# A cross network of six layers on one core: bank-to-bank PSUM copies, a second Strassen level in two products, and one rank list for the order

## The chip, the cores and the metric

One Trainium2 chip; the program runs on one of its cores. The metric is the device time in microseconds (us), as the median of several executions. A single-core program has no second die to compare with, so a run is called slow only when it lies over 1.5% above the fastest of the same kernel. "PE" is TensorE's matmul row in the trace, "PEld" its weight loads, "DVE" VectorE, "ACT" ScalarE, "SP" the queue that issues most DMAs.

## The reference

```python
B, F, D, L = 16384, 100, 16, 6
Din = min(F * D, 1024)                   # 1024
# x0: [B, Din], ws: [L, Din, Din], bs: [L, Din], all bfloat16
def reference(x0, ws, bs):
    x = x0
    for l in range(L):
        proj = jnp.einsum('bd,de->be', x, ws[l]) + bs[l]
        x = x0 * proj + x
    return x
```

Six products of 16384 x 1024 by 1024 x 1024, each followed by an elementwise step. The work is cut into 16 "pairs" of 1024 rows; a layer of a pair is called a **unit** here, so there are 96 units.

## The kernel before

Each unit is one product of two 1024 x 1024 matrices, done by Strassen's scheme in Winograd's form: seven products of 512 x 512 x 512 instead of eight, on sums of quadrants. The products are numbered 1 to 7; T1 to T4 are the sums of the quadrants of x, made by DVE; the sums of weights (5, 6, 7, 3) are made once, in pair 0, and kept in DRAM. One product is four *groups* (m = 0..3) of four matmuls with 512 columns. Product 2 is cut once more by the same scheme, into seven *inner groups* of four matmuls with 256 columns ("2i" are its sums of weights, "ti" its sums of x). This inner level saves an eighth of the columns of that one product.

```python
def group(pid, dst, m, start):                      # 4 matmuls, 512 columns each
    wt, rhs = weight(pid), rhs_of[pid]
    for k in range(KH):
        nc.tensor.matmul(dst[m][:], lhsT=wt[:, k, m * P:(m + 1) * P], rhs=rhs[:, k, :],
                         start=(start and k == 0), stop=(k == KH - 1), skip_group_check=True)
# ... one unit, in program order (cut) ...
for m in range(KH):                                  # product 1, bank pA[m]
    group(1, pA, m, True)
    evb(P1s[:, m, :], pA[m][:], 0, m)                # ACT: evict with bias
for m in range(KH):                                  # product 5, bank pX[m]
    group(5, pX, m, True)
    ev(P5s[:, m, :], pX[m][:])                       # ACT: evict
for m in range(KH):                                  # product 3 on top of product 5
    group(3, pX, m, False)
    evb(S53[:, m, :], pX[m][:], 0, m)
inner(1, 0, True); ev(i15[:, 0, :], pX[0][:])        # product 2, second level
inner(5, 1, True); ev(i15[:, 1, :], pX[1][:])
for m in (0, 1):
    group(6, pA, m, False)                           # product 6 on top of product 1
    ev(U2s[:, m, :], pA[m][:])
# ... inner 2, 6, 3, 7, 4 between the rest of products 6 and 7, 
#     each inner sum evicted by ACT and added by DVE ...
final(Q2[:], 0, 0)                                   # DVE: times x0, plus x
# ... product 7, product 4, their evictions, and the other three quadrants' finals ...
ti_next = emit_t(blk(xst, 1, 0))                     # DVE: inner sums for the next unit
emit_T(xst, Tn, (2, 3, 4))
```

PSUM has eight banks: `pA[0..3]` and `pX[0..3]`. Weights come through a ring of 14 tiles of 512 KB, eight loads per unit.

Of the kernel before, what the change touches and what calls it, by code (L numbers as in the profile page):

```python
# [1 line left out]

# [10 lines left out]
IDENT = mybir.ActivationFunctionType.Identity  # L13


@with_exitstack
def kernel(
# [18 lines left out]
    JB = PR // P  # L36

    KQ, HQ, NQ = KH // 2, H // 2, NB // 2

    const = ctx.enter_context(tc.tile_pool(name="const", bufs=1))  # L40
    dram = ctx.enter_context(tc.tile_pool(name="dram", bufs=1, space=bass.MemoryType.DRAM))
    x0t_pool = ctx.enter_context(tc.tile_pool(name="x0t", bufs=2))
    xst_pool = ctx.enter_context(tc.tile_pool(name="xst", bufs=2))
    t_pool = ctx.enter_context(tc.tile_pool(name="tp", bufs=1))
    ti_pool = ctx.enter_context(tc.tile_pool(name="tip", bufs=2))
    evi_pool = ctx.enter_context(tc.tile_pool(name="evi", bufs=1))
    ev_pool = ctx.enter_context(tc.tile_pool(name="evp", bufs=8))
    wring = ctx.enter_context(tc.tile_pool(name="wring", bufs=14))
    psum = ctx.enter_context(tc.tile_pool(name="ps", bufs=1, space=bass.MemoryType.PSUM))
    stage_ctx = ExitStack()  # L50
    w12_pool = stage_ctx.enter_context(tc.tile_pool(name="w12", bufs=2))
    xo_ctx = ExitStack()
    xo_pool = None

    Lc = dram.tile([L, 5, P, KH * H], BF16, name="Lc")
    CIDX = {5: 0, 6: 1, 7: 2, 3: 3, "2i": 4}
    pA = [psum.tile([P, NB], FP32, name=f"pA{i}") for i in range(KH)]
    pX = [psum.tile([P, NB], FP32, name=f"pX{i}") for i in range(KH)]

    def w_src(l, pid):  # L60
        wl = ws[l]
        if pid == 1:
            return wl[0:H, 0:H].rearrange("(k p) e -> p k e", p=P)
        if pid == 2:
            return wl[H:D, 0:H].rearrange("(k p) e -> p k e", p=P)
        if pid == 4:
            return wl[H:D, H:D].rearrange("(k p) e -> p k e", p=P)
        return Lc[l, CIDX[pid]].rearrange("p (k e) -> p k e", k=KH)

    ORDER = [1, 5, 3, 2, "2i", 6, 7, 4]  # L70
    all_keys = [(pr, l, pid) for pr in range(NPAIR) for l in range(L) for pid in ORDER]
    key_pos = {k_: i for i, k_ in enumerate(all_keys)}
    is_dma = lambda k_: not (k_[0] == 0 and k_[2] in CIDX)
    PREF = 11
    wtiles = {}
    state = {"next": 0}

    def prefetch_upto(n):
        while state["next"] < min(n, len(all_keys)):
            k_ = all_keys[state["next"]]  # L80
            if is_dma(k_) and k_ not in wtiles:
                wt = wring.tile([P, KH, H], BF16, name="wp")
                state["last_dma"] = nc.sync.dma_start(wt[:], w_src(k_[1], k_[2]))
                wtiles[k_] = wt
            state["next"] += 1
# [4 lines left out]
    def tt(out, in0, in1, op):  # L90
        nc.vector.tensor_tensor(out=out, in0=in0, in1=in1, op=op)  # L91

    def emit_T(xsrc, Ts, do):
        B11, B12, B21, B22 = blk(xsrc, 0, 0), blk(xsrc, 0, 1), blk(xsrc, 1, 0), blk(xsrc, 1, 1)
        for i in do:
            t_ = t_pool.tile([P, KH, NB], BF16, name=f"T{i}")
            Ts[i] = t_[:]
            if i == 1:
                tt(Ts[1], B12, B11, SUB)
            elif i == 2:  # L100
                tt(Ts[2], B22, Ts[1], SUB)
            elif i == 3:
                tt(Ts[3], B22, B12, SUB)
            else:
                tt(Ts[4], B21, Ts[2], SUB)

    def inner_w(t):
        v = t[:].rearrange("p q (k e) -> p q k e", k=KQ)
        return {5: v[:, 0], 6: v[:, 1], 3: v[:, 2], 7: v[:, 3]}

    def emit_t(B):
        q = lambda dh, n: B[:, dh * KQ:(dh + 1) * KQ, n * NQ:(n + 1) * NQ]
        t_ = ti_pool.tile([P, 4, KQ, NQ], BF16, name="ti")
        t1, t3, t2, t4 = (t_[:, i] for i in range(4))
        tt(t1, q(0, 1), q(0, 0), SUB)
        tt(t2, q(1, 1), t1, SUB)
        tt(t3, q(1, 1), q(0, 1), SUB)
        tt(t4, q(1, 0), t2, SUB)
        return {1: q(0, 0), 2: q(1, 0), 3: q(1, 1), 4: t4, 5: t1, 6: t2, 7: t3}

    combo_st = {}
    pending_saves = []

    def flush_saves():
        for (l_, pid_, t_) in pending_saves:
            si = nc.sync.dma_start(Lc[l_, CIDX[pid_]].rearrange("p (k e) -> p k e", k=KH), t_[:])
            if state.get("last_dma") is not None:
                tc.add_manual_dep(si.ins, state["last_dma"].ins.name,
                                  mybir.DependencyInfo(mybir.DependencyClass.NoSync, mybir.DependencyReason.DATA),
                                  reason="combo save behind the urgent weight loads")  # L130
        pending_saves.clear()

    def load_w12(l):
        st = combo_st.setdefault(l, {})
        if "w12" not in st:
            st["w12"] = w12_pool.tile([P, KH, H], BF16, name="w12")
            state["last_dma"] = nc.sync.dma_start(st["w12"][:], ws[l][0:H, H:D].rearrange("(k p) e -> p k e", p=P))
        return st["w12"]

    def emit_combo(l, pid):  # L140
        prefetch_upto(key_pos[(0, l, 4)] + 1)
        W11, W21, W22 = wtiles[(0, l, 1)], wtiles[(0, l, 2)], wtiles[(0, l, 4)]
        w12 = load_w12(l)
        t_ = wring.tile([P, KH, H], BF16, name="wp")
        if pid == 5:
            tt(t_[:], w12[:], W22[:], ADD)
        elif pid == 6:
            tt(t_[:], wtiles[(0, l, 5)][:], W11[:], SUB)
        elif pid == 3:
            tt(t_[:], W21[:], wtiles[(0, l, 6)][:], SUB)  # L150
        elif pid == 7:
            tt(t_[:], W11[:], w12[:], SUB)
        else:
            a11, a12 = W21[:, 0:KQ, 0:HQ], W21[:, KQ:KH, 0:HQ]
            a21, a22 = W21[:, 0:KQ, HQ:H], W21[:, KQ:KH, HQ:H]
            s = inner_w(t_)
            tt(s[5], a21, a22, ADD)
            tt(s[6], s[5], a11, SUB)
            tt(s[3], a12, s[6], SUB)
            tt(s[7], a11, a21, SUB)  # L160
        wtiles[(0, l, pid)] = t_
        pending_saves.append((l, pid, t_))

    wt0 = wring.tile([P, KH, H], BF16, name="wp")
    nc.sync.dma_start(wt0[:], w_src(0, 1))
    wtiles[(0, 0, 1)] = wt0
    load_w12(0)
    wt4 = wring.tile([P, KH, H], BF16, name="wp")
    nc.sync.dma_start(wt4[:], w_src(0, 4))
    wtiles[(0, 0, 4)] = wt4  # L170
    x0T_next = x0t_pool.tile([P, 2, KD, NB], BF16, name="x0T")
    for n in range(2):
        nc.sync.dma_start_transpose(out=x0T_next[:, n], in_=x0[n * NB:(n + 1) * NB, :])
    LK = L * KD
    b_bf = const.tile([P, LK], BF16, name="b_bf")
    nc.sync.dma_start_transpose(out=b_bf[:], in_=bs.rearrange("l (m p) -> (l m) p", p=P))
    b_all = const.tile([P, LK], FP32, name="b_all")
    prefetch_upto(8)
    nc.gpsimd.tensor_copy(b_all[:], b_bf[:])

    order_ctx = ctx.enter_context(tc.manual_schedule(engines={nc.tensor.engine, nc.scalar.engine, nc.vector.engine}))
    Tn = {}
    emit_combo(0, 5)
    emit_T(x0T_next, Tn, (1,))
    emit_combo(0, 6)
    emit_combo(0, 3)
    emit_combo(0, "2i")
    ti_next = emit_t(blk(x0T_next, 1, 0))
    emit_T(x0T_next, Tn, (2, 3))
    emit_combo(0, 7)  # L190
    emit_T(x0T_next, Tn, (4,))
    prefetch_upto(PREF)
    flush_saves()

    for pr in range(NPAIR):
        x0T = x0T_next
        xst = xst_pool.tile([P, 2, KD, NB], BF16, name="xst")
        last_pair = pr == NPAIR - 1
        xo_last = {"t": None, "regions": [], "xfin": None}

        def out_region(eh, n):
            if xo_last["t"] is None:
                xo_last["t"] = xo_pool.tile([P, 2, 2, KH, KH, P], BF16, name="xoS")
            ti = nc.sync.dma_start_transpose(out=xo_last["t"][:, eh, n].rearrange("p j k r -> p (j k) r"),
                                             in_=xo_last["xfin"][:, eh, n].rearrange("r j k p -> r (j k p)"))
            xo_last["regions"].append((eh, n))
            xo_last["tins"] = xo_last.get("tins", []) + [ti]

        for l in range(L):
            xsrc = x0T if l == 0 else xst  # L210
            Ts, ti = Tn, ti_next
            Tn = {}
            rhs_of = {1: blk(xsrc, 0, 0), 3: blk(xsrc, 1, 1), 4: Ts[4], 5: Ts[1], 6: Ts[2], 7: Ts[3]}
            bias_col = lambda eh, m: b_all[:, l * KD + eh * KH + m: l * KD + eh * KH + m + 1]
            last_layer = l + 1 == L
            combos_next = pr == 0 and not last_layer
            if combos_next:
                prefetch_upto(key_pos[(0, l + 1, 4)] + 1)
                load_w12(l + 1)
# [189 lines left out]
```

## Time and profile before

| kernel | median | runs |
|---|---|---|
| before | 2344.3 us | 2342.57 to 2345.61 (3 runs) |

The page's first part is the busy time of each engine, its share of the span, and the number of instructions.

```profile
span 2342.7 us, 31963 instructions
## 1 busy us (share of the span) xinstructions
PE 2277.5 (97%) x11668; PEld 1164.1 (50%) x11904; DVE 2003.2 (86%) x2160; ACT 1818.9 (78%) x2977; POOL 1.1 (0%) x5
```

The windows view, for the steady stretch: columns are the stretch, its length, then busy us and number of instructions for each engine, the granted clock, the share of the DMA engines' time, and GB/s.

```profile
200.00:2260.00 2060.00, 2048.66 (x10525) 1048.89 (x10736) 1775.60 (x1906) 1640.35 (x2685) 0.00 (x0) 1.00 0.75 222
```

PE is busy 99.4% of that stretch. The Trainium skill, "Trainium Kernel Development and Optimization", section "Performance Expectations", calls matmul busy time a bad metric for how close a kernel is to the roofline, because matmuls are pipelined. So I read starts instead. The timeline of before; each row is a start, a length, and merged like instructions:

```profile
1019.32 1.03 PE L233 MATMUL pX_92<-T_8766,wp 128*128 128x512 bf16 x4
1020.18 1.03 PE L233 MATMUL pX_93<-T_8766,wp 128*128 128x512 bf16 x4
...
1043.09 1.03 PE L233 MATMUL pX_92<-T_8891,wp 128*128 128x512 bf16 x4
```

Two groups of 512 columns start 0.86 us apart, although each row is 1.03 us long: the end of a matmul overlaps the next one. The same group of the next unit starts 23.77 us later. Groups cost 0.864 us and inner groups 0.437 us, from start to start, so 24 groups and 7 inner groups are 23.79 us: PE has no gap at all in a steady unit.

What isn't steady is the start. The waits of pair 0, from the timeline of PE (the bracket is the idle time before the row and what ended it):

```profile
11.80 1.86 PE L233 MATMUL pA_88<-x0T,wp 128*128 128x512 bf16 x4 [11.80 <-DMA x0T<-in_x_dram]
...
49.19 1.87 PE L233 MATMUL pA_88<-xst,wp 128*128 128x512 bf16 x4 [11.28 <-DVE xst L91]
```

Four more such waits, 0.95 to 3.6 us each, open the other layers of pair 0.

### The profile page before, as it was taken

Reading aid. Unit: us, or ns where it says so; the run is one execution under the profiler, and the core shown is the slowest. Engines: PE = TensorE matmul, PEld = TensorE weight load, DVE = VectorE, ACT = ScalarE, POOL = GpSimd, SP = SyncE. Lnnn points to the kernel's source line nnn. Section 1 sums busy time; section 2 is a strip of 40 time slices with the busy share of each in tenths; the row PEclk is TensorE's granted clock in tenths of the full one; section 3 lists DMA queues with packets and bytes.
Section 4 is the critical chain, followed back from the end, with each engine's and each line's share of the span. In section 5 each row is a group of like instructions: output and inputs, shape, how many; then the busy total and the mean of one; then the engine's idle time right before and its main releaser. Section 6 shows DMA issues by size and latency. Waiting matters only on the chain.

```text
span 2342.7 us, 31963 instructions
## 1 busy us (share of the span) xinstructions
PE 2277.5 (97%) x11668; PEld 1164.1 (50%) x11904; DVE 2003.2 (86%) x2160; ACT 1818.9 (78%) x2977; POOL 1.1 (0%) x5
## 2 busy tenths in 40 slices
PE   6989999999999999999999999999999999999996
PEld 2445555555454555555555545454555555554543
DVE  5998888888889788888888888888898888988886
ACT  4767777878787787778787878778777777787775
POOL 0000000000000000000000000000000000000000
PEclk8999999999999999999999999999999999999998
DMA  7659669595785958759586695967859578595853
GB/s 242 198 198 239 229 193 267 182 257 198 206 256 185 274 187 213 252 178 284 174 222 240 189 276 171 254 206 207 253 189 271 193 204 257 175 284 178 234 191 81
DMA packets 613837, 508.60 MB, mean 217 GB/s; under 512 B 399664, under 2 KB 552240, under 8 KB 613680
## 3 DMA queue, kind: packets, MB, share of 16 engines
q1 hardware_dynamic: 613680, 506.53, 72.5%
q8 instruction: 95, 1.56, 0.3%
q14 instruction: 62, 0.51, 0.1%
HBM read 390.07 MB, written 49.28 MB: 188 GB/s over the span
## 4 chain that ended last, share of the span: by engine, by line
PE 87%; DVE 10%; issue 1%; ACT 1%; SPq 1%; DMA 0%; DVEq 0%
PE pA_91 L233 13%; PE pA_88 L233 13%; PE pA_89 L233 13%; PE pA_90 L233 12%; PE pX_92 L245 7%; PE pX_94 L233 6%; PE pX_93 L233 6%; PE pX_95 L233 6%; PE pX_92 L233 6%; DVE ev L91 4%; PE pX_93 L245 3%; DVE xst L91 2%; PE pX_94 L245 2%; DVE wp L91 1%; DVE ti L91 1%
## 5 line engine op out<-in xcount | busy, mean ns | idle before, releaser
L233 PEld LDWEIGHTS <-wp 128*128 128x128 bf16 x9216 | 901.4, 98 | 1026.5 <-issue 55.1
L91 DVE TENSOR_TENSOR ev<-ev,x0T 128x2048 bf16<-128x2048 bf16 x384 | 469.8, 1223 | 9.9
L91 DVE TENSOR_TENSOR xst<-ev,xst 128x2048 bf16<-128x2048 bf16 x320 | 384.9, 1224 | 21.7 <-DVE ev L91 0.5
L91 DVE TENSOR_TENSOR ev<-ev 128x2048 bf16<-128x2048 bf16 x288 | 352.2, 1223 | 38.0 <-ACT ev L249 25.7
L245 PEld LDWEIGHTS <-wp 128*128 128x128 bf16 x2688 | 262.7, 98 | 133.2
L252 ACT ACTIVATE ev<-pA_88,b_all 128x512 bf16<-128x512 f32 x288 | 198.4, 689 | 69.9 <-PE pA_88 L233 65.7
L252 ACT ACTIVATE ev<-pA_90,b_all 128x512 bf16<-128x512 f32 x288 | 198.1, 688 | 34.9 <-PE pA_90 L233 33.4
L252 ACT ACTIVATE ev<-pA_91,b_all 128x512 bf16<-128x512 f32 x288 | 197.9, 687 | 34.0 <-PE pA_91 L233 34.0
L252 ACT ACTIVATE ev<-pA_89,b_all 128x512 bf16<-128x512 f32 x288 | 198.3, 689 | 25.6 <-PE pA_89 L233 1.8
L245 PE MATMUL pX_92<-ti,wp 128*128 128x256 bf16 x1152 | 172.8, 273 | 1.1
L249 ACT CAST ev<-pX_92 128x512 bf16<-128x512 f32 x192 | 112.3, 585 | 28.8 <-PE pX_92 L233 16.7
L233 PE MATMUL pA_88<-xst,wp 128*128 128x512 bf16 x320 | 83.0, 382 | 22.4 <-DVE xst L91 22.4
L252 ACT ACTIVATE ev<-pX_92,b_all 128x512 bf16<-128x512 f32 x96 | 66.0, 687 | 26.6 <-PE pX_92 L233 24.3
L233 PE MATMUL pA_89<-xst,wp 128*128 128x512 bf16 x314 | 83.2, 385 | 0.3
L233 PE MATMUL pA_91<-xst,wp 128*128 128x512 bf16 x315 | 82.3, 381 | 0.6
L233 PE MATMUL pX_94<-xst,wp 128*128 128x512 bf16 x320 | 82.1, 379 | 0.3
L233 PE MATMUL pA_90<-xst,wp 128*128 128x512 bf16 x306 | 81.7, 385 | 0.4
L233 PE MATMUL pX_93<-xst,wp 128*128 128x512 bf16 x308 | 80.5, 379 | 0.7
L233 PE MATMUL pX_95<-xst,wp 128*128 128x512 bf16 x308 | 80.5, 379 | 0.3
L233 PE MATMUL pX_92<-xst,wp 128*128 128x512 bf16 x306 | 80.3, 379 | 0.4
L252 ACT ACTIVATE ev<-pX_93,b_all 128x512 bf16<-128x512 f32 x96 | 66.0, 687 | 16.9 <-PE pX_93 L233 15.7
L252 ACT ACTIVATE ev<-pX_94,b_all 128x512 bf16<-128x512 f32 x96 | 66.0, 687 | 16.9 <-PE pX_94 L233 16.9
(2831 smaller groups left out, 3586.4 us busy)
## 6 DMA issues: line engine op xcount, KB each, us to landing
wp<-Lc SPq DMA_DIRECT2D x450, 512.0 KB, 4.3
wp<-in_ws_dram SPq DMA_DIRECT2D x288, 512.0 KB, 4.9
out_dram<-x0T SPq DMA_DIRECT2D x30, 1024.0 KB, 10.2
Lc<-wp SPq DMA_DIRECT2D x30, 512.0 KB, 6.3
out_dram<-xoS SPq DMA_DIRECT2D x4, 512.0 KB, 4.7
w_98<-in_ws_dram SPq DMA_DIRECT2D x1, 512.0 KB, 5.0
x0T<-in_x_dram SPq DMA_TRANSPOSE x32, 7.3
w_151<-in_ws_dram SPq DMA_DIRECT2D x1, 512.0 KB, 5.4
```

The source lines that it names most:

```text
L91: nc.vector.tensor_tensor(out=out, in0=in0, in1=in1, op=op)
L233: nc.tensor.matmul(dst[m][:], lhsT=wt[:, k, m * P:(m + 1) * P], rhs=rhs[:, k, :], start=(start and k == 0), stop=(k == KH - 1), skip_group ...
L245: nc.tensor.matmul(dst[:, m * NQ:(m + 1) * NQ], lhsT=wv[:, k, m * P:(m + 1) * P], rhs=ti[i][:, k, :], start=(start and m == 0 and k == 0), ...
L249: nc.scalar.copy(out=dst, in_=src)
L252: nc.scalar.activation(out=dst, in_=src, func=IDENT, bias=bias_col(eh, m), scale=1.0)
```

## The change

The intent has three parts.

1. **A second Strassen level inside two products, 5 and 2**, instead of in 2 alone. A steady unit then has 20 groups and 14 inner groups: 23.39 us of PE instead of 23.79. Pair 0 and the last unit drop the second level and have 28 groups, 24.18 us.
2. **Bank-to-bank copies.** A sum that two results share is copied by ACT from one PSUM bank to another (`F`, `f1`, `f2`), and PE goes on accumulating in both, so that DVE need not add the two.
3. **One rank list.** Every operation of PE, ACT and DVE has a rank, roughly its wanted start time in the unit; all operations are put out in order of rank as soon as what they depend on has been put out. Each engine works strictly in that order.

The diff, cut to its core (`...` marks cuts; the old unit's body is removed whole):

```diff
+R2 = ranks("""                      # two-level units; "name@rank"
+P1.0@0 5p1@.9 5p5@1.3 P1.1@1.7 P1.2@2.6 5p2@3.5 5p6@3.9 2p1@4.3 2p5@4.8 P1.3@5.2 5p3@6.1 5p7@6.5 2p2@7 2p6@7.4
+5p4@8 P6.1@8.5 2p7@9.4 P6.0@9.8 P3.1@10.7 2p3@11.5 2p4@12 P3.0@12.4 P6.3@13.3 P6.2@14.1 P3.3@15 P3.2@15.9
+P7.3@16.7 P7.0@17.6 P7.2@18.4 P7.1@19.3 P4.3@20.2 P4.0@21 P4.2@21.9 P4.1@22.8
+5e_p5@2 5f1@2.6 E1.1@3.1 E1.2@3.7 5e_c11@4.2 E1.0@4.7 5f2@5.3 2e_p5@5.7 2f1@6.4 5e_c12@6.8 5e_u3@7.3 2e_c11@7.8
+2f2@8.4 E1.3@8.9 F.1@9.6 5e_c21@10 2e_u3@10.5 F.0@11 2e_c12@12.2 E3.1@12.7 2e_c21@13.2 E3.0@13.7 F.3@14.3
+F.2@15.2 E3.3@16.1 E3.2@16.9 E7.3@17.8 E7.2@19.5 E7.0@20.1 E7.1@20.7 E4.0@22.1 E4.3@22.7 E4.2@23.2 E4.1@23.8
+T1@-1.1 5t13@.2 5t2@2.1 2t13@3.7 5t4@5.4 2t2@6.9 T2@7.2 T4@8.5 T3@9.6 2t4@10.8 5cc@11.1 2cc@12.8 Q1@13.9 Qm@15.1
+Qa@16.4 Ua@17.6 Um@18.9 Ux@20.2 Va@21.4 Wm@24.6 Wx@26 Vm@27.9 Vx@29.4
+""")
...
+SPAN2, SPAN0 = 23.4, 24.2           # length of a unit in ranks
...
-    wring = ctx.enter_context(tc.tile_pool(name="wring", bufs=14))
+    wring = ctx.enter_context(tc.tile_pool(name="wring", bufs=RING))      # 16
...
+    level1 = lambda u: units[u][0] == 0 or u == NU - 1
...
+                inner(5, b, True)                                # products 5 and 2, second level
+                copy(X + "e_p5", ip5[X][:], v3(b), [Xn[b]], [X + "ps"])
+                inner(1, a, True)
+                copy(X + "f1", pX[b][:], pX[a][:], [Xn[a]], [Xn[b]])   # bank to bank
+                inner(2, b, False)
+                copy(X + "e_c11", c(0, 0), v3(b), [Xn[b]], cn(0, 0))
+                inner(6, a, False)
+                copy(X + "f2", pX[b][:], pX[a][:], [Xn[a]], [Xn[b]])   # bank to bank
+                inner(3, b, False)
+                copy(X + "e_c12", iu[X][:, 0], v3(b), [Xn[b]], [X + "u0"])
+                inner(7, a, False)
+                copy(X + "e_u3", iu[X][:, 1], v3(a), [Xn[a]], [X + "u1"])
+                inner(4, a, False)
...
+        for m in range(KH):
+            xb = m if one else m % 2
+            group(f"P6.{m}", "6", pA[m], A[m], T[2], ["T2", A[m]], m, False)
+            copy(f"F.{m}", pX[xb][:], pA[m][:], [A[m]], [Xn[xb]])      # bank to bank
+            group(f"P3.{m}", "3", pX[xb], Xn[xb], B22, [XI[1, 1], Xn[xb]], m, False)
...
+    heap = [(ops[i][0], i) for i in range(len(ops)) if need[i] == 0]
+    heapq.heapify(heap)
+    while heap:
+        _, i = heapq.heappop(heap)
+        ops[i][1]()
...
```

Names: `P6.1` is group m = 1 of product 6, `E3.1` and `E7.1` are evictions, `F.1` a copy from bank to bank, `5p4` is the fourth inner product of product 5, `T2` a sum of quadrants, `5t4` an inner sum. `Q, U, V, W` are the four quadrants of the result; the suffixes are DVE steps: `a` or `1` adds, `m` multiplies by x0, `x` adds x (`Qa` is Q's last). Small parts of the change: x0 is loaded in four quarters at the start, 24 matmuls of zeros warm PE up (in the changed kernel's trace the first matmuls start 0.427 us apart, those from about 5.4 us on 0.216), the sums of weights are saved by the GpSimd queue.

The zeros do something else, too. The Trainium skill, "PSUM — Partial Sum Buffer", section "The four PSUM rules", says that writes of ScalarE neither set nor clear the bits which decide whether a matmul accumulates, that a matmul adds to what ScalarE wrote where an earlier matmul has left the bit set, and that zero is the only such start value that is safe either way. Accumulating on a copied bank relies on the bit being set.

## The prediction

> **What bounds it now.** The tensor engine's stream of columns. In the page's engine totals PE is busy 97% (DVE 86%, ACT 78%); by windows, 99.4% from 300 us to 2300 us. In the timeline a 4-matmul group of 512 columns starts every 0.864 us and an inner group of four 256-column matmuls every 0.437 us. One layer of one pair ("unit", 96 of them) is 24 and 7 of these: 23.79 us; the timeline shows 23.77 between like groups. 96 units are 2283 us. The other 60 us are: 11.8 us before the first matmul, 4 us of slow first groups, 22 us of PE waits on DVE at the starts of pair 0's layers (11.3, 0.95, 3.3, 3.3, 3.6), and 18 us after the last matmul. Steady units have none.
>
> **What changes.** 89 units get a second inner product in place of P5: 20 groups and 14 inner groups, 23.39 us (-0.40). Seven units (pair 0 and the last) go to one level: 28 groups, 24.18 us (+0.40). Net PE: -32 us (1.4%), all of it on the critical path, if PE stays the limit. Reordering should recover pair-0 waits.
>
> **What it adds per steady unit.** DVE: 15 adds of 2048 (1.14 us start to start, 1.26 where dependent), four of 1024 (estimated 0.60), four of 512 (0.34): about 22.1 us, 94% of 23.4. ACT: 16 biased evictions (0.58 to 0.69) and 18 copies (0.47 to 0.58): 18 to 21 us. Ten copies go from bank to bank; the Trainium skill, "ScalarE: Activation LUTs", in "Step-by-step: what each stage is for" says PSUM is the quicker destination; no trace here shows it yet. Weight loads: 9 of 512 KB instead of 8, 202 GB/s instead of 176; DMA busy rises from 72% to about 80%, with peaks at pair boundaries.
>
> **Why I don't grant the whole gain.** In rank order there is a loop across units: P6.1 waits for T2 of this unit; P6.1 to the start of P4.1 is 15 groups and 3 inner groups, 14.27 us; start of P4.1 to its eviction's end and Wm 1.81 us (1.07 + 0.69 + 0.05); then DVE, in order, Wm, 5t2, Wx, 2t13, Vm, 5t4, Vx, 2t2 before T2, 6.3 us; T2 to PE 1.37 us (1.23 + 0.14, as at the layer starts of pair 0). Sum 23.76 us, an estimate. So PE should wait 0.2 to 0.4 us before P6.1 in every unit; P6.3 -> copy -> P3.3 is also tight, within 0.1 us. I expect 23.5 to 23.8 us per unit, middle 23.68: nearly all of the PE saving turns into a wait.
>
> **Sum.** First matmul of data at 7 to 8 us; pair 0, near-balanced between PE and DVE (24.2 to 24.8 us a unit, plus about 8 us of startup waits), ends at about 163 us (182 before); 89 x 23.68 = 2107; last unit 24.5; tail 18.5. Total 2313 us, -1.3%; range 2288 to 2338. Chances: faster by over 2% 0.24, within 2% 0.74, slower by over 2% 0.02.
>
> **What would show it.** Steady period by the timeline; in the waits, PE pA <- DVE T2 of 0.2 to 0.4 us some 89 times; first-slice and pair-0 windows about 19 us shorter; the 1024-wide broadcast add near 0.69 us long; bank-to-bank copies at or below 0.585 us; no PE wait on DMA.
>
> **What would make it wrong.** Period 23.4 (loop hidden): 2289. The broadcast add losing its fast rate (1.2 us): DVE becomes the limit, 2330 or more. Weight loads late at pair boundaries: +1 us per pair. GpSimd saves slowing DVE in pair 0.

## The result, and the profile after

| kernel | median | runs | ratio to before, fast runs | 95% |
|---|---|---|---|---|
| before | 2344.31 us | 2342.57 to 2345.61 (4) | 1 | |
| changed | 2319.18 us | 2318.4 to 2320.84 (4) | 0.9894 | 0.988 to 0.9908 |

Ratios here and below are the mean time of one kernel's fast runs over that of the kernel before's in the same rounds, so not quite the ratio of the medians. The change wins 1.1%, clear of noise.

The same two views of the changed kernel:

```profile
span 2316.6 us, 34627 instructions
## 1 busy us (share of the span) xinstructions
PE 2272.3 (98%) x12674; PEld 1261.3 (54%) x12912; DVE 2102.9 (91%) x2218; ACT 1837.5 (79%) x3223; POOL 20.4 (1%) x41
```

```profile
200.00:2260.00 2060.00, 2048.18 (x11630) 1156.40 (x11846) 1901.77 (x2004) 1683.99 (x2962) 0.00 (x0) 1.00 0.80 243
```

PE's busy share of the steady stretch is 99.4% again, before and after, and after it hides a quarter of a microsecond of waiting in every unit. This fits the skill's warning: the row of a group here is longer (1.03 or 0.60 us) than its 0.864 or 0.437 us share of the stream, so a short wait falls inside the row and the profile doesn't count it. Only starts show it. The timeline of the changed kernel, one unit (its P1.0 starts at 1017.97):

```profile
1024.04 0.60 PE L287 MATMUL pX<-T,wp 128*128 128x256 bf16 x4
1024.48 0.60 PE L287 MATMUL pX<-ti,wp 128*128 128x256 bf16 x4
1025.04 0.60 PE L287 MATMUL pX<-x0T,wp 128*128 128x256 bf16 x4
1025.47 1.16 PE L287 MATMUL pX<-ti,wp 128*128 128x256 bf16 x8
1026.47 1.03 PE L189 MATMUL pA<-T,wp 128*128 128x512 bf16 x3
...
1041.60 1.03 PE L189 MATMUL pA<-xst,wp 128*128 128x512 bf16 x4
```

The rows are 5p3, 5p7, 2p2, then 2p6 and 5p4 together, P6.1, and P1.0 of the next unit, 23.63 us after this one's. 2p2 starts 0.56 us after 5p7 where 0.44 is its due; P6.1 starts 1.00 us after 2p6 where two inner groups take 0.87. I matched the single matmul records to the program's order through the weight loads (whose records are complete) and averaged over 70 steady units: the period is 23.655 us; **0.123 us is lost before 2p2, 0.120 us before 5p4, 0.012 us before P6.1**, 0.013 and 0.007 us before P3.3 and P3.2, nothing elsewhere. The rest, 23.38 us, is PE's own stream (23.39 by the sum above).

What 2p2 and 5p4 wait for is on ACT. Its timeline in the same unit:

```profile
1019.91 0.58 ACT L194 CAST ip<-pX 128x512 bf16<-128x512 f32 x1 [1.04 <-PE pX L287]
1020.52 0.57 ACT L194 COPY pX<-pX 128x512 f32<-128x512 f32 x1
1021.00 1.32 ACT L198 ACTIVATE ev<-pA,b_all 128x512 bf16<-128x512 f32 x2
1022.22 0.58 ACT L194 CAST ev<-pX 128x512 bf16<-128x512 f32 x1
1022.68 0.70 ACT L198 ACTIVATE ev<-pA,b_all 128x512 bf16<-128x512 f32 x1
1023.26 0.61 ACT L194 COPY pX<-pX 128x512 f32<-128x512 f32 x1
1023.78 0.61 ACT L194 CAST ip<-pX 128x512 bf16<-128x512 f32 x1
1024.42 0.57 ACT L194 COPY pX<-pX 128x512 f32<-128x512 f32 x1
1024.90 1.08 ACT L194 CAST iu<-pX 128x512 bf16<-128x512 f32 x2
```

These are 5e_p5, 5f1, E1.1 and E1.2, 5e_c11, **E1.0 at 1022.68**, 5f2, 2e_p5, 2f1, then 5e_c12 and 5e_u3. The bank copy 2f1 ends at 1024.99, and 2p2, which accumulates on that copy, starts at 1025.04. The eviction 5e_u3 ends at 1025.98; by the matched records 5p4, which goes on in the bank that it reads, starts on average 8.06 us into the unit, here 1026.03. ACT waits 1.04 us for PE before 5e_p5; from there to the end of this list it is never idle for more than about 0.03 us. This is no chance of one unit: over 80 steady units 2p2 starts 0.052 us after the end of 2f1, and 5p4 0.052 us after the end of 5e_u3, each within 0.001.

The other candidate is on DVE, which the prediction had named: T2, for which P6.1 waits. The timeline of DVE:

```profile
1018.89 1.23 DVE L103 TENSOR_TENSOR ev<-ev,x0T 128x2048 bf16<-128x2048 bf16 x1
...
1024.72 0.42 DVE L103 TENSOR_TENSOR ti<-x0T,ti 128x512 bf16<-128x512 bf16 x1
1025.05 2.55 DVE L103 TENSOR_TENSOR T<-x0T,T 128x2048 bf16<-128x2048 bf16 x2
```

Wm starts at 1018.89, 0.03 us after the eviction of P4.1 (a group of the unit before) has ended, as it does in nearly every steady unit. T2 (the first of the two merged) starts at 1025.05 and ends at 1026.27, and P6.1 starts at 1026.47. Where PE is seen to wait for T2, as in experiments 1 and 4, P6.1 starts 0.053 us after its end; here it is 0.089 us on average, so T2 comes some 0.04 us before it is needed. Two chains, then, end within some hundredths of a microsecond of each other.

Where the time came from, by the starts of unit 0, of unit 6 (pair 1) and of the last unit in both timelines:

| stretch | before | changed | difference |
|---|---|---|---|
| up to the first matmul of data | 11.8 | 8.4 | -3.4 |
| pair 0 (6 units) | 171.9 | 155.9 | -16.0 |
| 89 steady units | 2116.6 (23.78 each) | 2107.2 (23.68) | -9.4 |
| last unit | 23.8 | 24.3 | +0.6 |
| after the last matmul | 18.6 | 20.7 | +2.1 |
| span | 2342.7 | 2316.6 | -26.1 |

Three quarters of the gain is in the first 164 us. Of the 35 us that the second level saves on PE in the steady units (89 x 0.40), 9.4 us arrive.

### The profile page after: what moved, and what is told of

It reads as the page before. It is cut to its first block, busy times and chain, and to the rows that moved or that the text cites. A ratio compares the mean times of both kernels' runs of the same rounds, so it can differ in the third digit from the quotient of the medians.

```text
span 2316.6 us, 34627 instructions
## 1 busy us (share of the span) xinstructions
PE 2272.3 (98%) x12674; PEld 1261.3 (54%) x12912; DVE 2102.9 (91%) x2218; ACT 1837.5 (79%) x3223; POOL 20.4 (1%) x41
## 4 chain that ended last, share of the span: by engine, by line
PE 95%; DVE 2%; issue 1%; DMA 1%; SPq 0%; ACT 0%; DVEq 0%; ACTq 0%
PE pA L189 55%; PE pX L287 24%; PE pX L189 16%; DVE ev L103 1%; DVE xst L103 1%; SPq L384 0%; DVE T L103 0%; DMA Lc<-isum 0%; DMA x0T<-in_x_dram 0%; DVE wp L103 0%; ACT ev L198 0%; DVE ti L103 0%; SPq L391 0%; DVE isum L103 0%; ACT pX L194 0%
## 5 line engine op out<-in xcount | busy, mean ns | idle before, releaser
L189 PE MATMUL pA<-T,wp 128*128 128x512 bf16 x4512 | 1051.8, 379 | 5.5 <-DVE T L103 0.4
L198 ACT ACTIVATE ev<-pA,b_all 128x512 bf16<-128x512 f32 x1124 | 720.0, 688 | 187.9 <-PE pA L189 187.9
L103 DVE TENSOR_TENSOR ev<-ev,x0T 128x2048 bf16<-128x2048 bf16 x384 | 469.7, 1223 | 9.9 <-ACT ev L198 2.3
L287 PE MATMUL pX<-ti,wp 128*128 128x256 bf16 x2848 | 423.1, 272 | 1.6 <-DVE ti L103 1.6
L103 DVE TENSOR_TENSOR ev<-ev,ev 128x2048 bf16<-128x2048 bf16 x281 | 344.2, 1225 | 47.7 <-ACT ev L194 33.1
L189 PE MATMUL pX<-xst,wp 128*128 128x512 bf16 x1328 | 334.5, 378 | 4.9 <-DVE xst L103 2.2
L198 ACT ACTIVATE ev<-pX,b_all 128x512 bf16<-128x512 f32 x412 | 284.1, 694 | 54.8 <-PE pX L189 46.7
L189 PE MATMUL pA<-xst,wp 128*128 128x512 bf16 x1203 | 302.2, 379 | 4.0
L194 ACT COPY pX<-pA 128x512 f32<-128x512 f32 x412 | 239.9, 587 | 69.5 <-PE pA L189 66.7
L194 ACT CAST ev<-pX 128x512 bf16<-128x512 f32 x384 | 227.5, 595 | 0.3 <-PE pX L189 0.2
L194 ACT COPY pX<-pX 128x512 f32<-128x512 f32 x356 | 206.2, 579 | 8.5
```

Source lines behind the costliest of these rows:

```text
L103: nc.vector.tensor_tensor(out=o, in0=a, in1=b, op=op)
L189: nc.tensor.matmul(bank[:], lhsT=wt[(u, w)][:, k, m * P:(m + 1) * P], rhs=rhs[:, k, :], start=(start and k == 0), stop=(k == KH - 1), skip ...
L194: add(name, lambda: nc.scalar.copy(out=dst, in_=src), rd, wr)
L198: add(name, lambda: nc.scalar.activation(out=dst, in_=src, func=IDENT, bias=b_all[:, c:c + 1], scale=1.0), rd, wr)
L287: nc.tensor.matmul(pX[bank][:, m * NQ:(m + 1) * NQ], lhsT=wv[:, k, m * P:(m + 1) * P], rhs=rhs[:, k, :], start=(start and m == 0 and k == ...
```

## The experiments

All are edits of the changed kernel, with all else the same. Every kernel "agreed with the reference"; one of them (p6_t1) computes something else on purpose and agreed too. That test is loose here: computed from the reference's inputs (1024 rows of them), the six layers together add 0.6% of x0's root mean square.

### 1. An extra addition on DVE, just before T2, and elsewhere

```diff
+        if not one:
+            ttop("pad", padt[:], zeros[:], zeros[:], ADD, [], ["pad"])
 # pad_loop: pad@7.05 (before T2@7.2)        pad_gap: pad@11.6 (after 5cc@11.1, where DVE idles)
```

> One extra DVE add of 512 elements (0.34 us start to start) is put into every two-level unit just before T2, with a correct result. Theory (a loop across units sets the 23.65 us period: P6.1 waits for T2, T2 for the DVE queue from Wm on, Wm for the eviction of P4.1, and P4.1 for P6.1): the period grows by the whole 0.34 us to 23.99, 89 times, so 2319 -> about 2349 us. Rival 1 (DVE is simply full): the same +30 us. Rival 2 (the 0.26 us over PE's own 23.39 comes from PE, from PSUM or from the weight loads): 2319, because DVE has over 1 us of idle time per unit.

> The same extra add, but placed after the first broadcast add (5cc), where DVE idles 0.95 us per unit. Theory of the loop: this place is not on the loop, period stays 23.65, 2319 us. Rival 1 (DVE full): +30 us as in the other place. Rival 2: 2319.

| run | median | ratio to before | period |
|---|---|---|---|
| pad_loop | 2345.39 us | 1.0006 | 23.952 |
| pad_gap | 2319.05 us | 0.9893 | 23.652 |

The same instruction costs 26 us in one place and nothing in the other. So DVE isn't simply full, although it is busy 91% of the span; its place in the order is what counts. In pad_loop the wait before P6.1 has become long enough for the profile to count some of it:

```profile
534.73 1.02 PE L190 MATMUL pA<-T,wp 128*128 128x512 bf16 x4 [0.15 <-DVE T L104]
```

By the matched records the wait before P6.1 rose from 0.012 to 0.311 us, so the 0.34 us went into the loop all but for 0.04. This shows that there is next to no slack before T2. It doesn't show that a shorter way to T2 would help; the next run asks that. (The periods of pad_gap and of the changed kernel, 23.652 and 23.655, also show how little a period read in this way scatters.)

### 2. P6 reads another operand (wrong)

```diff
-            group(f"P6.{m}", "6", pA[m], A[m], T[2], ["T2", A[m]], m, False)
+            group(f"P6.{m}", "6", pA[m], A[m], T[2] if one else T[1], ["T2" if one else "T1", A[m]], m, False)
```

> Wrong result on purpose: in two-level units the matmuls of P6 read T1, which is ready long before, instead of T2; nothing else moves. Theory of the loop: the wait before P6.1 (0.13 us visible) is gone, the other visible gap (0.12 us before 2p2, a wait for a bank-to-bank copy) stays, period 23.39 + 0.12 = 23.51, about 2306 us. Rival 1 (DVE full) and rival 2 (PE, PSUM, loads): no change, 2319.

Measured: 2317.35 us (0.9888), period 23.639. My theory, that the loop through T2 alone sets the period, missed: it had promised 13 us, and 2 came. The timeline of this kernel has the same gap as before, with no T2 to wait for:

```profile
528.58 1.16 PE L287 MATMUL pX<-ti,wp 128*128 128x256 bf16 x8
529.58 1.03 PE L189 MATMUL pA<-T,wp 128*128 128x512 bf16 x4
```

The start distance is 1.00 us again. The matched records put the loss before 5p4, the second of the two groups in the merged row (0.123 us there, none before P6.1). The loop through T2 is real, as the extra addition showed, but something else is as long. (The "0.13 us visible" of the expectation was this same loss before 5p4, read wrongly as a wait before P6.1.)

### 3. A rank edit that was to fill a hole on DVE

```diff
-... 2t13@3.7 5t4@5.4 2t2@6.9 ...
+... 2t13@3.7 5t4@3.3 2t2@6.9 ...
```

> A correct result and the same instructions; one rank number changes, 5t4 from 5.4 to 3.3, so that DVE does this 512-element add between Wx and 2t13. 2t13 depends on Wx and starts 1.32 us after it where an independent op starts after 1.14, so the add fills 0.18 us in which DVE stood. Theory of the loop: Wm to T2 is 0.15 to 0.18 us shorter in the five of six units where the input is not x0, period about 23.51, about 2307 us, and the before-P6.1 gap goes. Rival 1 (DVE full): also some gain. Rival 2: 2319.

Measured: 2322.45 us (0.9908), period 23.688: 3 us slower, a miss. The timeline of DVE in this kernel tells why:

```profile
549.14 1.22 DVE L103 TENSOR_TENSOR ev<-ev,x0T 128x2048 bf16<-128x2048 bf16 x1
...
552.69 1.22 DVE L103 TENSOR_TENSOR ev<-ev,x0T 128x2048 bf16<-128x2048 bf16 x1
554.02 1.23 DVE L103 TENSOR_TENSOR xst<-ev,xst 128x2048 bf16<-128x2048 bf16 x1
555.16 0.42 DVE L103 TENSOR_TENSOR ti<-xst,ti 128x512 bf16<-128x512 bf16 x1
555.50 2.55 DVE L103 TENSOR_TENSOR T<-xst,T 128x2048 bf16<-128x2048 bf16 x2
```

With 5t4 gone from between Vm (552.69) and Vx (554.02), Vx follows the operation that it depends on and starts 1.33 us after it instead of the 1.14 of an independent one. 5t4 had been filling that hole, and the other hole was smaller than I had read from one unit: in the changed kernel 2t13 starts 1.25 us after Wx in 51 of 68 steady units with x as input, and 1.32 in 14. From Wm to T2 is 6.36 us here and 6.28 in the changed kernel. The period rose, which is the direction that the loop gives for a longer stretch.

### 4. Two limits: each taken away alone, and both together

The new theory: two limits lie within hundredths of each other. Limit 1 is ACT's chain of bank copies and evictions, which costs PE 0.24 us before 2p2 and 5p4. Limit 2 is the loop through T2. The first edit moves one eviction into ACT's idle time; the second halves T2, so that P6.1 can begin on its first half.

```diff
 # e10_early
-... 5e_c11@4.2 E1.0@4.7 5f2@5.3 ...
+... 5e_c11@4.2 E1.0@1.2 5f2@5.3 ...
 # t2_split
-        ttop("T2", T[2][:], B22, T[1][:], SUB, [XI[1, 1], "T1"], ["T2"])
+        def t2(B22=B22, one=one):
+            for k in ((0, KH // 2), (KH // 2, KH)) if not one else ((0, KH),):
+                tt(T[2][:, k[0]:k[1]], B22[:, k[0]:k[1]], T[1][:, k[0]:k[1]], SUB)
+        add("T2", t2, [XI[1, 1], "T1"], ["T2"])
 # t2_e10: both
```

> Correct result; one rank number: the eviction of P1.0 (E1.0) goes on ACT from 4.7 to 1.2, where ACT idles about 1 us, so that the chain of copies behind it (5f2, 2e_p5, 2f1, 5e_c12, 5e_u3) starts 0.4 us earlier. New theory, from the trace of the changed kernel and of p6_t1: two limits tie at 23.65 us. Limit 1 is local: PE waits 0.12 us before 2p2 for the bank copy 2f1 and 0.12 us before 5p4 for the eviction 5e_u3. Limit 2 is the loop through T2. Alone, this edit takes limit 1 away and leaves limit 2: both waits vanish, a wait of about 0.25 us shows up before P6.1, period 23.64, 2318 us (within 2). Rival (only the ACT chain limits, and the tie is chance): period 23.41, about 2297 us.

> Correct result; T2 is computed by two DVE adds of 1024 (k 0 and 1, then k 2 and 3) instead of one of 2048 in the two-level units, so the first two matmuls of P6.1 can start 0.55 us earlier; the loop through T2 is about 0.35 us shorter. Theory of the two tied limits: limit 1 (ACT chain, 0.24 us before 2p2 and 5p4) is left, period 23.63 to 23.65, 2317 to 2319 us. Rival (only the T2 loop limits): period 23.40, about 2297 us.

> Both edits together, correct result. Theory of the two tied limits: neither limit is left, PE streams without a wait but for some 0.02 us before P3.3 and P3.2, period 23.41, 89 x 0.24 = 22 us less than the changed kernel, about 2297 us. If the two limits were not both real, this would equal one of the single edits.

| run | median | ratio | period | lost before 2p2 | 5p4 | P6.1 |
|---|---|---|---|---|---|---|
| changed | 2319.18 us | 0.9894 | 23.655 | 0.123 | 0.120 | 0.012 |
| e10_early | 2314.58 us | 0.9877 | 23.610 | 0 | 0.010 | 0.199 |
| t2_split | 2316.9 us | 0.9888 | 23.639 | 0.123 | 0.121 | 0 |
| t2_e10 | 2296.53 us | 0.9800 | 23.407 | 0 | 0.011 | 0 |

By the ratios, which take out the drift of 1 us between rounds, the edits alone are worth 4 and 1 us, and together 22; 89 times the differences of the periods gives the same. Alone each lies within the intervals of the ratios, so it is the periods that show them; together they are far outside. In e10_early the ACT waits are gone and the wait before P6.1 is there instead; the timeline, where the row of 2p2 now follows 5p7 by 0.43 us, and P6.1 follows 2p6 by 1.09:

```profile
527.09 0.60 PE L287 MATMUL pX<-ti,wp 128*128 128x256 bf16 x4
527.52 0.60 PE L287 MATMUL pX<-xst,wp 128*128 128x256 bf16 x4
527.96 1.05 PE L287 MATMUL pX<-ti,wp 128*128 128x256 bf16 x8
529.05 1.02 PE L189 MATMUL pA<-T,wp 128*128 128x512 bf16 x4
```

In e10_early P6.1 starts 0.053 us after the end of T2 in every steady unit, while 2f1 ends 0.35 us before 2p2. With both edits the distance from 2p6 to P6.1 falls to 0.89 us, next to the 0.87 of the stream:

```profile
524.99 1.05 PE L290 MATMUL pX<-ti,wp 128*128 128x256 bf16 x8
525.88 1.03 PE L189 MATMUL pA<-T,wp 128*128 128x512 bf16 x4
```

So both limits are shown. The loop alone allows about 23.61 us (e10_early), the ACT chain alone about 23.64 (t2_split), PE alone 23.39. The changed kernel runs at the longest of them, but for 0.015 us. With both edits PE's stream stands at its own 23.39 but for 0.02 us, so no third limit is left in a steady unit.

### 5. The order and the bank copies without any second level

```diff
-    level1 = lambda u: units[u][0] == 0 or u == NU - 1
+    level1 = lambda u: True
```

> Correct result; the second Strassen level is taken out of every unit and the new order and the bank copies stay (28 groups of 512 columns per unit). It tells what the order and the start alone are worth. PE needs 28 x 0.864 = 24.18 us per unit; if bank copies and order cost PE nothing, the steady period is 24.2 and the time 2319 + 89 x 0.53 - 2 = about 2364 us, and the first 164 us are as in the changed kernel. If the copies cost PE time, the period is above 24.3 and the time above 2373 us.

Measured: 2378.27 us (1.0149). The period is 24.34 in the unit shown (24.33 on average), not 24.18, so the time lies 14 us above the expectation (89 x 0.16). PE's timeline shows where:

```profile
1016.43 3.62 PE L189 MATMUL pA<-xst,wp 128*128 128x512 bf16 x16
1020.05 3.61 PE L189 MATMUL pX<-xst,wp 128*128 128x512 bf16 x16
1023.50 3.62 PE L189 MATMUL pX<-T,wp 128*128 128x512 bf16 x15
...
1040.77 3.62 PE L189 MATMUL pA<-x0T,wp 128*128 128x512 bf16 x16
```

Product 1 takes 3.62 us until product 2 begins, the other products 3.45: this order waits 0.16 us for the start of product 2. The trace tells what for. In the five layers whose input is not x0, product 2 starts 0.147 us after the end of Wx, the DVE operation that makes its x, in nearly every steady unit; in four of these layers the copy of the bank has by then been over for 0.2 us. Only where the input is x0 does it wait for the copies alone, 0.13 us in all. So it is mostly the order, not the copies, that costs this run its 14 us. The first 164 us are about the same as in the changed kernel. Against the 23.66 of the changed kernel, its second level in two products is worth 59 us, of which those 14 are the waits of this other order; and because one_level keeps the better start and is still slower than before, the start alone doesn't pay for losing the second level.

### 6. One bank copy undone

```diff
-            copy(f"F.{m}", pX[xb][:], pA[m][:], [A[m]], [Xn[xb]])
-            group(f"P3.{m}", "3", pX[xb], Xn[xb], B22, [XI[1, 1], Xn[xb]], m, False)
+            if one:
+                copy(f"F.{m}", pX[xb][:], pA[m][:], [A[m]], [Xn[xb]])
+            else:
+                copy(f"F.{m}", S6[:, m, :], pA[m][:], [A[m]], [f"S6.{m}"])
+            group(f"P3.{m}", "3", pX[xb], Xn[xb], B22, [XI[1, 1], Xn[xb]], m, not one)
...
+            ttop("Ub", U[:], U[:], S6[:], ADD, allm("U") + allm("S6"), allm("U"))      # two-level units
```

> One part of the change undone on the changed kernel, correct result: in the two-level units the sum P1 + P6 is not copied to another bank for P3 to accumulate on; ACT evicts it to SBUF instead (same number of ACT operations), P3 starts its bank anew, and DVE adds the two (one more add of 2048, 1.14 to 1.26 us, between the eviction of P3 and T2). Theory of the loop: that add is on the loop (from the eviction of P3.2 through DVE to T2), so the period grows by 0.9 to 1.2 us, 2319 + 80 to 107 = 2400 to 2425 us. Rival (DVE has 1.3 us idle per unit, so an add of 1.2 us fits): within 10 us of 2319.

Measured: 2408.18 us (1.0271), period 24.67, 89 us above the changed kernel: inside what the loop gives, and far from the rival. The rival had counted 1.3 us of idle DVE time per unit, but that time lies after T2, not where the addition is needed. By the matched records 0.48 us is now lost before 5p1, for T1, 0.36 before 5p5 and 0.19 before P6.1: the longer DVE queue already holds PE up before it comes to T2. The profile counts part of it:

```profile
1006.24 0.60 PE L288 MATMUL pX<-T,wp 128*128 128x256 bf16 x4 [0.32 <-DVE T L104]
1007.04 0.60 PE L288 MATMUL pX<-ti,wp 128*128 128x256 bf16 x4 [0.20 <-DVE ti L104]
```

So the copy to another bank is what lets this order stand: it takes an addition of 1.2 us off DVE, and the ACT operation stays one either way.

### 7. Around the faster version: the start, and the end

Three kernels on top of t2_e10.

```diff
 # t2_e10_bias: the load of the biases before the last quarter of x0
+    nc.sync.dma_start_transpose(out=b_bf[:], in_=bs.rearrange("l (m p) -> (l m) p", p=P))
+    nc.gpsimd.tensor_copy(b_all[:], b_bf[:])
     load_quarter(1, 1)
 # t2_e10_dummy8: fewer matmuls of zeros
-    NDUMMY = 24
+    NDUMMY = 8
 # best: t2_e10_bias, and a rank list for the last unit alone, with P3 before P7
+RLAST = {**R0, **ranks("""
+...
+P3.2@13.9 P3.0@14.7 P3.1@15.6 P3.3@16.4 P7.2@17.3 P7.0@18.2 P7.1@19 P7.3@19.9
+... Ua@18.4 Um@19.6 Ux@20.8 Va@22 Vm@23.2 Vx@24.4 Wm@25.3 Wx@26.5 """)}
```

> On top of t2_e10 (2296.5 us); correct result. The load of the biases is issued before the last quarter of x0 instead of after it. In the trace PE waits 4.8 to 5.5 us at 21 us for the biased eviction of P2, which waits for the biases. Theory A (that wait is on the critical path): the first product P5 starts at about 18.5 us and 2.5 us are won, 2294. Theory B (the start is limited by DVE and by the loads of the second layer's weights, seen in the 2 to 3 us PE wait for DVE at 46 us): that wait grows by what the first one lost, 2296 to 2296.5.

> On top of t2_e10; correct result. 8 matmuls of zeros before the first data instead of 24 (one for each bank; with none, the check refuses the kernel because the first accumulating matmul would meet banks that no matmul has touched). If the warm-up is worth nothing, because PE then waits for the biases anyway: 2296.5, with the first groups of data at 1.7 us instead of 0.86. If it is worth what those groups lose: up to 2 us more, 2298.5.

> t2_e10 with the early bias load and another rank list for the last unit alone (P3 before P7, so that DVE is not left with eight operations after the last matmul); correct result. The tail from the last matmul to the end, 20.8 us in the changed kernel, should fall by about 3 us: 2291 to 2293.5 us.

| run | median | before in the same rounds | ratio |
|---|---|---|---|
| t2_e10 (earlier rounds) | 2296.53 us | 2343.48 | 0.9800 |
| t2_e10_bias | 2299.15 us | 2345.08 | 0.9805 |
| t2_e10_dummy8 | 2298.88 us | 2345.08 | 0.9803 |
| best | 2293.9 us | 2345.08 | 0.9784 |

The early biases win nothing. Their wait at 20 us fell from 4.78 to 3.38 us, and a later one grew; the timeline of PE, first of t2_e10 and then of t2_e10_bias:

```profile
46.38 3.61 PE L189 MATMUL pX<-xst,wp 128*128 128x512 bf16 x16 [2.89 <-DVE xst L103]
```

```profile
46.12 6.17 PE L189 MATMUL pX<-xst,wp 128*128 128x512 bf16 x16 [3.78 <-DMA wp<-in_ws_dram]
```

The gain went into that later wait, as theory B had it, though the profile now names a load of weights where it named DVE. There is a second cost: after the 3.78 us of waiting the next 16 matmuls took 6.17 us instead of 3.61. Twelve of them start about 0.427 us apart, as the first matmuls of the program do, instead of 0.216; the granted clock from 46 to 50 us is 0.50. The smaller warm-up changed little either: its first 16 matmuls of data took 5.31 us instead of 3.62, and PE waited for the biases afterwards as before. Both differences from t2_e10 (0.0005 and 0.0003 in ratio) are within the intervals.

The other order in the last unit is clear against t2_e10_bias of the same rounds, from which it differs in nothing else: 5 us, where I had expected 3 (2293.9 is a little above the range given, because the early biases had won nothing). In the timeline of "best" the last block of 32 matmuls starts at 2268.68 and so ends at 2275.6, 16 us before the end of the span, where the changed kernel has 20.7. "best" beats the kernel before by 2.2% (interval 0.977 to 0.9799) and the changed kernel by 1.1%.

## Why the prediction was right, and where it was not

The time was right, 2313 us said and 2319.2 measured, in the range and in the class. Term by term:

| term | predicted | measured |
|---|---|---|
| first matmul of data | 7 to 8 us | 8.4 |
| end of pair 0 | 163 us | 164.3 |
| 89 units | 23.68 us each, 2107 | 23.68 each, 2107.2 |
| last unit | 24.5 us | 24.3 |
| tail | 18.5 us | 20.7 |

**"Nearly all of the PE saving turns into a wait"** was right: of 0.40 us per unit 0.26 are waited away at the steady period of 23.655. The sum was right for half a reason, though.

**"PE should wait 0.2 to 0.4 us before P6.1 in every unit"** is the step that failed. That wait was 0.012 us. The losses were 0.123 us before 2p2 and 0.120 us before 5p4, and they came from ACT's chain of copies in a queue that is idle about 20% of the time: PE waited for ACT, not for DVE. I had looked at ACT's busy share and cleared it. What I should have walked through is the order of its queue from 5e_p5 to 5e_u3: a row of operations about 0.5 to 0.6 us apart from start to start, with PE waiting at the end of the row, and one of them (E1.0) not urgent at all.

**The loop itself** was real but too long by my sum: 23.76 us predicted, 23.61 measured when it was the only limit (e10_early). The term that was mis-sized most is "T2 to PE 1.37": T2 takes 1.22 us and P6.1 starts 0.053 us after its end, 1.27 in all, where I had taken the 0.14 us of the layer starts of pair 0. With P4.1 to Wm at 1.79 and Wm to T2 at 6.28 us the sum is 23.61. The extra addition lengthened the loop by nearly its whole length. That the wrong limit gave the right number was luck: the two limits happened to be nearly equal.

**"P6.3 -> copy -> P3.3 is also tight, within 0.1 us"**: 0.013 us before P3.3 in the trace. Right, and of no weight.

**"The 1024-wide broadcast add near 0.69 us"**: 688 ns. The group of the page:

```profile
L103 DVE TENSOR_TENSOR ev<-iu,ip 128x1024 bf16<-128x1024 bf16 x178 | 122.5, 688 | 85.9 <-ACT iu L194 85.9
L194 ACT COPY pX<-pX 128x512 f32<-128x512 f32 x356 | 206.2, 579 | 8.5
L194 ACT CAST ip<-pX 128x512 bf16<-128x512 f32 x178 | 106.1, 596 | 94.2 <-PE pX L287 94.2
```

The columns are busy us, the mean ns of one, and idle us before them. The Trainium skill, "VectorE: DVE Perf Modes", section "The perf-mode tier table", gives 1224 ns for an add of 2048 bf16 elements; the trace has 1223. The add of 1024 with a repeated operand (stride 0 outside) is no longer than an ordinary one of 1024: 5t13 and 2t13 take 0.68 to 0.69 us in the timelines.

**"Bank-to-bank copies at or below 0.585 us"**: 579 ns within pX, 587 from pA to pX, 2 ns too long, against 595 to 596 to SBUF in the same kernel. These means mix two cases. Where ACT was idle just before, a copy to PSUM takes 570 ns and one to SBUF 585; in a full queue both take 594 to 607 on average. The direction that the skill's page on ScalarE gives is there in the first case alone, with 15 ns, and the copies to SBUF also turn fp32 into bf16, which no run here parts from the place.

**"No PE wait on DMA"** held in the steady units: the waits of PE in the whole run name DVE and ACT alone. **The tail** was short by 2.2 us, because I took the tail of before; in the rank order of the last unit DVE had more left to do after the last matmul. **"GpSimd saves slowing DVE in pair 0"** isn't seen: adds of 2048 take 1.221 us there on average and 1.222 later.

What stays open: how much of the 16 us won in pair 0 belongs to the missing second level, how much to the order and how much to the saves from another queue. No run parts them.

## What to carry to other kernels

When one engine streams without a gap and is made faster, walk the in-order queues of the others operation by operation, and add up every closed chain that leads from a group of one unit to the same group of the next; a queue that is 80% busy can still cost a quarter of a microsecond in each unit, as ACT did here. When removing the limit that you believe in gives nothing, look for a second one of equal length before you drop the first: remove both, and read the waits from the distances between starts, since a wait shorter than the overlap of two matmul rows isn't in any busy or idle total. An addition of a known size at two places of the same queue tells whether a place is on such a chain; whether shortening the chain pays is another question, which only a run that shortens it answers.

## What the Trainium skill lacked or had wrong

- "Trainium Kernel Development and Optimization" ("Performance Expectations") is right that matmul busy time misleads, but doesn't say how short waits hide: here PE's busy total was 2048.66 and 2048.18 us of the same 2060 us in two kernels, one without waits and one with 0.26 us per unit. The distance between the starts of groups, 0.864 and 0.437 us without a wait, shows them.
- "ScalarE: Activation LUTs" ("Step-by-step: what each stage is for") calls PSUM the quicker destination and gives no size there: for 128 x 512 read as fp32 it was 570 ns to PSUM as fp32 and 585 ns to SBUF as bf16 where ACT had been idle, and no difference showed in a full queue (594 to 607 ns both ways).
- "VectorE: DVE Perf Modes" has the length of an add (1224 ns; 1223 measured), but no page has what an add that needs the result of the one just before it costs from start to start: 1.25 to 1.33 us for 2048 elements, against about 1.14 for an independent one.
- No page has the cost of handing work between engines in a running stream, as read here: 1.07 us from the start of a group of four matmuls to the start of its eviction (0.86 of it is the group), 0.03 us from an eviction's end to DVE and 0.05 to PE, and from an add's end to PE 0.05 us (T2 to P6.1) or 0.15 (Wx to product 2 in one_level), a difference that no run here explains.
